# Attention weights change partitions through DRAM in 5 transfers a pair instead of 16, under a new order of all steps

## The chip, the cores and the metric

The kernel runs on one core of one Trainium2 chip. The metric is the device time of one execution in microseconds (us). Three runs of the kernel before took 381.66, 388.07 and 1155.09 us, with a median of 388.07 us. The execution that was profiled took 381.47 us; all rows below are from that one.

The core has five engines with a program of their own: TensorE (PE in the rows; PEld is its weight load), VectorE (DVE), ScalarE (ACT), GpSimd (POOL) and SyncE (SP). SP issues all the DMAs of this kernel. Each engine works through its instructions in the order in which they were written.

## The reference

```python
# attention: batch 4, 8 heads, 768 positions, head_dim 64, chunks of 32 positions, 8 memory keys
for c in range(nc):
    l_start, r_end = max(0, 32 * c - 16), min(S, 32 * c + 32 + 8)
    k_full = np.concatenate([mem_k, k[:, :, l_start:r_end]], axis=2)
    v_full = np.concatenate([mem_v, v[:, :, l_start:r_end]], axis=2)
    scores = scale * np.matmul(q_c, k_full.transpose(0, 1, 3, 2))
    a = np.exp(scores - np.max(scores, axis=-1, keepdims=True))
    a = a / (np.sum(a, axis=-1, keepdims=True) + 1e-09)
    out[:, :, 32 * c:32 * c + 32] = np.matmul(a, v_full)
# then x = that, as [batch, position, 512], and a gated block
h = gelu(x @ w_in)                                   # 512 -> 1024
u, v = h[..., :512], h[..., 512:]
v_n = (v - mean(v)) / np.sqrt(var(v) + 1e-06) * g_ln
v_s = np.einsum('ts,bsd->btd', w_sg, v_n) + b_sg[None, :, None]
return x + (u * v_s) @ w_out                         # 512 -> 512
```

All is float32. The large products run on TensorE as three products each of a high and a low part.

## The kernel before, in words

The work is cut into 24 attention units u: batch b = u // 6 and a tile of 128 positions, four chunks of 32. The names of steps below are those of the table ORDER (line 33), the letter or letters of a step with its unit or block behind them.

For each unit, **k** and **v** load its queries, keys and values (640 and 512 KB). **S** makes the scores on TensorE: 32 matmuls in the program, which the trace counts as 64, each with a weight load. **mx, sb, ex, sm, sr, nm** make the softmax on DVE, ACT and POOL; the weights of a unit stand in the tile `na`, 128 positions by 512. For the values they must stand with the keys on the partitions. Units 0 to 9 do that with four TensorE transposes (**T**) and a copy (**p**). Units 10 to 23, that is the pairs 5 to 11, do it in two moves: **yt** on DVE transposes blocks of 32 by 32 within their own 32 partitions into the tile `y`, and once both units of a pair are there, **Ea, Eb, Ec, Ed** bring the blocks to their partitions with four DMAs of 32 KB each, SBUF to SBUF (`pt<-y` in the rows). **A** then multiplies the weights in `pt` with the values: again 32 matmuls in the program and 64 in the trace, with as many weight loads. **xc, xh, xl** bring the result into the tiles `x` and `pair`.

The gated block follows for each batch: **V** (six) and **U** (eight) are the products with w_in, **W** (batch 0) or **P** (28 smaller products for each other batch) that with w_sg, **R** (14) that with w_out, **o** adds it to x, **out** stores a tile. **r, d** load and split the weights at the start. Blocks of w_sg and w_out that were prepared once go to DRAM (`blocks`, `outw`) and come back per batch into four ring tiles (**L**, 1152 KB each, and **M**, 512 KB each). An L or M waits until the product that last read its place in the ring has ended.

All steps stand in one hand-kept list. The loop at the end of `conformer_kernel` goes through ORDER and writes each step to its engine; a star chooses the step's second engine. Each engine, and the DMA queue on SP, keeps that order. What waits for what follows from the tiles. So the list decides what TensorE does next, and a DMA on SP whose wait isn't over holds up all DMAs listed behind it. The tiles `y` and `pt` exist once: E of a pair waits until A of the pair before has read `pt`, and the next yt waits until the transfers have read `y`.

Of the kernel before, what the change touches and what calls it, by code (L numbers as in the profile page):

```python
# [38 lines left out]
d2i01* S6 z5 d3i03 v500 d1i01 sr4 nm4* v502 vx00 d1i03 A3 v4 T4 vx02 vy02 sm5 d3i01 g31 p4 xc3 d4i03 d4i01 d4i00
xh3 d5i00 d4i02 xl3* sr5 nm5 Vb01 k7 v101 v602 S7 d5i01 A4 d6i01* k8 vy00 v600 d1o2* V03 mx7 d6i00* mx6 xh4 sb7  # L40
T5 d5i03 cb sb6 v702* v5 k9 g40 d5i02 ex6 d6i03* U001 xl4 v501 g01 p5 d2o2 d3o2 d6i02 v700* A5 v802 v6 xh5 v902*
d4o2 g00 Co10* xl5 g51 z6 ex7 S8 ga40 mx8 u1001 Co30 sm6 sm7 g50 v103 sr6 v800 V04 d5o2 Co20* d5o0 nm6 vx01
d6o2* v503 v7 g20 V05 k10 Co40* d6o0 v104 ga31 v900* v504 vy01 v105 v601 sr7 S9 sb8 v505 T6 ga21 hso0 lso0* nm7*
vx05 g10 xc4 mx9 g30 sb9 U011 v701* ga30 vx04 k11 U010 gb40 vx03 u1011 ex8 S10 Y00 xc5 p6* ex9 ro1 sm8 T7 vy03
v603 ga20 v703 g41 gb20* ga50 U002 sr8 vy05 p7 ga10 v803 mx10 vy04 U013 nm8 gb10* v605 v903* v604 d2o1 u1013
sb10 k12 ga00 u1002 gb50* d3o1 Y01 A6 v8 v705 v704* d1o1* sm9 v805 gb30 A7 gb00* xc6 ro3 gb31* v905* S12 v9 ga01
v801 g11 U003 T8 d4o1 v901* v804 N1 u1003 v904* d1o3 d5o1 U000 u1000 d2o3 ga11 d3o3 u1010 d4o3 d5o3 W002 W003
ga51 Co11 Co21 p8 Co31* d6o3* Co41 sr9 N0 Ga0 d6o1 nm9* hso1 W000 gb01 lso1* w1002 w2002 w1000 xc7 gb21* ga41
S11 Y10 Gd0 mx11 Gc0 sb11 A8 gb41 ex11 w1003 gb11 Gb0 Y11 H30 H10 gb51 I10 H20 W001 J10* w1001 k13 Ga1 I30 w2003
I20 H40* w2000 ex10 M01 W010 I40 sm10 J20 z11 Gb1 T9 U012 J40 sr10 Gd1 w3003 K20 xc8 nm10* w1010 Gc1 mx12 p9  # L50
sb12 w2001 u1012 sm11 w3001 K10 W012 J30 M06 ex12 H31* w2010 w3002 sr11 I31 H11* w3000 I11 w1012 w4002* yt10 H21
H41 I41 K30 w4000* K40 nm11 Ht100 It100 w4003* I21 M00 v10 M03 W013 w4001 W011 J21 J11 J41* A9 k14 w2012 Gb2
w1013 Gc2 J31 Ht300* w1011 yt11 Gd2 w2011 S13 K21 w2013 R100 Ed5 Ht101 R101 Ga2 It101 R201 o101 o201 o100 w3013
R200 o200 K41 Jt100 K31 w3012 K11 Jt101 Ec5 xh7 R501 xh6 o501 Ht301 xh8 w4013 k15 R500 w4012 Ht200* R301 o500
o301 z12 sm12 H32 M04 H12 S14 xl7* Ea5 xl6 R300 o300 sr12 I32 It200 I12 J32 V10 v110 mx14 V11 Ht201* It201 J12*
xl8* V12 Jt200* k16 H22 H42* I22 I42 nm12 sb14 Jt201* J42 v112 K12 v111 Eb5 v512 v511 Ht400* ex14 R600 J22 vx12
R601 K32 K42 M05 v510 vx11 It300 K22 o600 U101 S16 Jt300 Ht401 sm14 It301 A10 mx13 sb13 Jt301 o601 vy12 sr14
vy11 U102 vx10 ex13 It401 sm13 It400 M02 mx16 Jt400 Jt401* R700 o700 yt12 R701 R400 o701 R401 u1102 k18 v611
o400 S15 v11 out000 out001 o401 mx15 sr13 nm13 yt13 v711* U103 u1103 U100 v612 out002 out003 xc9 xh9 A11 vy10
sb15 xl9* xc11 nm14 out011 C311 sb16 v12 xh11 v610 xl11* xc10 xh10 xl10* V13 v113 out012 U111 u1100 v710* ex16  # L60
v513 C310* vx13 V14 L10 vy13 v613 v713 C110 C210 ex15 v813 sm15 k17 Ed6 C410 v810 v712 v910* sr15 S18 S17 mx17
v114 v913* v514 vx14 V15 Ec6 U110 sm16 out013 out010 vy14 v614 Ea6 v115 v515 v13 vx15 U112 vy15 v714 Eb6 L13
hs10 L11 ls10* u1112 v615 u1110 A13 C111 C312 v715 C112* v812 C211 v811 yt14 nm15 u1111 v815 C212 v912 A12 sr16
u1101 v911* sb17 v15 v814 C411* U113 u1113 P110 k19 yt15 ex17 v914* C412* v915* k20 P111 Q111 P210 P211 S19 L14
hs12 Q110 z17 L15 sm17 ls12 w1101 mx18 hs11 ls11 P611 P610 Q611 w2101 w3101 Q610 w4101* P711 Q711 P710 w1100
w2100 w3100 Ea7 w4100* P511 w1113 P510 nm16* sr17 sb18 Q710 xc12 w1112 w2113* P311 w2112* ex18 w3112 L16 xc13
w3113 P310 w1111 w2111 w1110 Ec7 w2110 M10 w4113* mx19 P411 Ht111* It111 Ht110* It110 R111 P410 Ht311 It311 M13
S20 Ht310* Eb7 Ed7 w1103 A15 v14 Jt111 yt16 w1102 M11 A14 nm17* w2103 w3103 Jt110* M16 yt17 k22 w2102 It310
Ht211* R110 It211 w4112 xc14 Ht210 k21 R510 w4103 o510 R511 w3102 R310 Jt310 sb19 w4102 o511 o110 o310 R311 M14
z18 N2 R211 It210 o311 R210 Jt210* Ed8 Ht410* M12 It410 xh12 xh14 xh13 Jt211 S21 o111 o211 xl12* R611 M15 R610  # L70
o210 V20 v120 xl14* xl13 V21 mx20 o610 v520 Ht411* Ea8 v17 sm18 sr18 It411 Jt410 Eb8 o611 Jt311 R710 o710 v121
v521 R711 Ec8 o711 Jt411 R410 R411 vx21 V22 vx20 nm18* U200 vy20 v620 o410 o411 sb20 ex20 out101 ex19 v122 v16
yt18 sm19 sr19 out100 mx21 v720* out113 C320 out102 out103 xc15 xh15 xl15* S22 A17 A16 nm19* V23 vy21 L21 v621
# [20 lines left out]
It231 Jt231 w4302 out212 Jt130* R130 M33 M31 w1303 w2303 R531 It331 o131 o531 R530 It330 M36 o530 M34 R331 R330
w3303 w4303 M35 Ht230 It230 Jt230 o331 R231 o130 Ht431 M32 o330 R630 R631 o231 out301 R230 o630 out310 Jt331
Jt330* R730 o631 o230 Ht430* o730 It431 Jt431 It430 R731 o731 Jt430 R430 R431 out300 out311 out312 out313 o430
out302 o431 out303
"""


# [831 lines left out]
```

## Time and profile before

| what | value |
|---|---|
| runs | 381.66, 388.07, 1155.09 us |
| the profiled execution | 381.47 us, its span 379.6 us |
| mean granted clock of TensorE | 0.986 |
| TensorE busy | 349.2 us, 92% of the span |
| weight loads busy (beside the matmuls) | 324.2 us, 85% |
| DVE, ACT, POOL busy | 266.5, 175.2, 202.5 us |
| chain that ended last | PE 80%, DMA 9%, issue 3%, ACT 3%, DVE 3% |
| DMA | 100.60 MB, mean 265 GB/s |

The span runs from the first to the last instruction; the execution's own time lies 1.9 us above it. The chain is followed back from the last instruction, at each step to what released it. "Issue" is time in which an engine waited for nothing that the profile shows. The granted clock is 1.00 at 2.4 GHz and 0.50 at 1.2 GHz.

### The profile page before, as it was taken

What the parts mean: (1) busy time and instruction counts of PE and PEld (TensorE: products, weight loads), DVE (VectorE), ACT (ScalarE), POOL (GpSimd) and SP (SyncE); (2) the same over time, 40 slices, a digit from 0 to 9 for tenths busy, and PEclk for the clock granted to TensorE, in tenths of its full rate; (3) what the DMA queues carried; (4) which work ended last, traced back from release to release, by engine and by line L of the source; (5) the groups of instructions that cost most, each with busy time, mean ns of one, the idle gap of its engine ahead of it and who ended that gap; (6) DMA issues with size and microseconds to landing.
All of it is one profiled execution on the core that took longest, in us unless ns stands there. A gap on an engine that the chain in (4) does not pass through costs nothing.

```text
span 379.6 us, 11105 instructions
## 1 busy us (share of the span) xinstructions
PE 349.2 (92%) x4678; PEld 324.2 (85%) x4678; DVE 266.5 (70%) x474; ACT 175.2 (46%) x299; POOL 202.5 (53%) x212
## 2 busy tenths in 40 slices
PE   2469989999999999999997995999999999999996
PEld 1349878889999888899987894899999998899996
DVE  2599998958788767795693773477477752655794
ACT  2366878745744543753251452774323423441140
POOL 1445877926848546065285551357348253452593
PEclk9999999999999999999998997899999999999999
DMA  7999688998996898489877677561994579008854
GB/s 272 355 372 382 230 298 273 305 354 302 329 376 241 281 350 308 149 319 385 306 265 268 210 214 294 197 246 39 325 377 177 182 233 403 12 0 310 318 174 169
DMA packets 33729, 100.60 MB, mean 265 GB/s; under 512 B 5264, under 2 KB 16016, under 8 KB 30736
## 3 DMA queue, kind: packets, MB, share of 16 engines
q1 hardware_dynamic: 33680, 99.90, 73.7%
q8 instruction: 37, 0.61, 0.7%
q14 instruction: 12, 0.10, 0.1%
HBM read 77.99 MB, written 18.22 MB: 253 GB/s over the span
## 4 chain that ended last, share of the span: by engine, by line
PE 80%; DMA 9%; issue 3%; ACT 3%; DVE 3%; POOL 2%; SPq 0%; ACTq 0%; POOLq 0%
PE mmc L109 19%; PE mmb L109 18%; PE mmd L109 17%; PE mma L109 16%; PE av L109 6%; PE s L109 4%; DMA qka<-in_qks 3%; DMA rawc<-in_w_in 2%; DMA ringa<-blocks 2%; DMA work<-in_w_out 2%; POOL gd L109 1%; ACT L109 1%; DVE mxb L109 1%; POOL work L109 0%; DVE ea L109 0%
## 5 line engine op out<-in xcount | busy, mean ns | idle before, releaser
L109 ACT ACT_TABLE_LOAD x24 | 30.8, 1283 | 5.5 <-DVE ea L109 2.8
L109 POOL TENSOR_TENSOR sums<-work,sums 128x384 fp32r<-128x384 f32 (+2 forms) x15 | 18.6, 1255 | 11.5 <-ACT sums L109 11.4
L109 ACT CAST sums<-work 128x384 fp32r<-128x384 f32 (+3 forms) x25 | 16.1, 662 | 13.2 <-DVE work L109 9.8
L109 PE MATMUL s<-qka 64*32 64x64 f32 x768 | 11.4, 246 | 7.7 <-DMA qka<-in_qks 6.8
L109 PEld LDWEIGHTS s<-qka 64*32 64x32 f32 x768 | 9.3, 116 | 10.0 <-DMA qka<-in_qks 4.7
L109 PE MATMUL av<-pt,vb 64*64 64x32 f32 x704 | 13.2, 220 | 4.1 <-issue 4.1
L109 PEld LDWEIGHTS av<-pt,vb 64*64 64x64 f32 x704 | 11.9, 135 | 5.6 <-issue 5.2
L109 PEld LDWEIGHTS av<-pt,va 64*64 64x64 f32 x768 | 13.6, 142 | 3.3 <-ACT pt L109 1.7
L109 PE MATMUL av<-pt,va 64*64 64x32 f32 x768 | 14.9, 226 | 1.4 <-ACT pt L109 1.4
L109 ACT ACTIVATE ea<-ea 128x512 f32<-128x512 f32 x12 | 7.6, 633 | 13.1 <-DVE ea L109 13.0
L109 POOL TENSOR_TENSOR work<-work 128x384 f32<-128x384 f32 (+1 forms) x6 | 6.7, 1109 | 11.8 <-DMA uh<-in_w_sgT 7.5
L109 POOL TENSOR_SCALAR rsb<-mvb 128x1 f32<-128x1 f32 x8 | 2.4, 299 | 19.3 <-DVE mvb L109 15.6
L109 PE MATMUL s<-qkb 64*32 64x64 f32 x704 | 10.1, 240 | 2.3 <-DVE ea L109 1.5
L109 PEld LDWEIGHTS s<-qkb 64*32 64x32 f32 x704 | 8.3, 112 | 4.4 <-DVE ea L109 1.8
L109 DVE TENSOR_TENSOR sums<-work,sums 128x768 fp32r<-128x768 f32 (+2 forms) x10 | 9.7, 966 | 2.1 <-ACT sums L109 2.1
L109 DVE STREAM_TRANSPOSE y<-na 128x512 f32<-128x512 f32 x14 | 9.9, 704 | 0.3 <-DMA qka<-in_qks 0.2
L109 PE MATMUL mmb<-w_in_hi,pairb 128*128 128x512 f32 x32 | 10.0, 439 | 0.0
L109 PE MATMUL mmd<-w_in_hi,paira 128*128 128x512 f32 (+1 forms) x40 | 10.0, 376 | 0.0
L109 DVE TENSOR_REDUCE mxa<-s 128x8 f32<-128x512 f32 x8 | 5.4, 677 | 6.3 <-PE s L109 6.3
L109 POOL TENSOR_SCALAR rsa<-mva 128x1 f32<-128x1 f32 x8 | 1.8, 224 | 14.8 <-DVE mva L109 14.5
L109 ACT ACTIVATE eb<-eb 128x512 f32<-128x512 f32 x12 | 7.5, 629 | 3.9 <-DVE eb L109 3.9
L109 PE MATMUL mmc<-w_in_hi,paira 128*128 128x512 f32 (+1 forms) x40 | 9.2, 351 | 0.0
(773 smaller groups left out, 1226.8 us busy)
## 6 DMA issues: line engine op xcount, KB each, us to landing
qka<-in_qks SPq DMA_DIRECT2D x12, 640.0 KB, 6.8
qkb<-in_qks SPq DMA_DIRECT2D x11, 640.0 KB, 6.2
ringd<-blocks SPq DMA_DIRECT2D x6, 1152.0 KB, 6.8
ringb<-blocks SPq DMA_DIRECT2D x6, 1152.0 KB, 6.7
va<-in_vs SPq DMA_DIRECT2D x12, 512.0 KB, 5.7
ringa<-blocks SPq DMA_DIRECT2D x5, 1152.0 KB, 6.5
vb<-in_vs SPq DMA_DIRECT2D x11, 512.0 KB, 5.2
ringa<-outw SPq DMA_DIRECT2D x11, 512.0 KB, 6.0
```

What stands on the lines that cost most here:

```text
L109: return self.tc.keep_in_program_order(getattr(self.engine, name)(*args, **kw))
```

## The change

Two things change. First, the four steps Ea to Ed of a pair (16 DMAs) become two: **X** writes the tile `y` to a DRAM tile `exch` of the pair's own, with four DMAs of 128 KB, and **E** reads it back into `pt` with one DMA of 512 KB. Second, the list ORDER is another one throughout, and the second engine is chosen for other steps. The products are the same.

```diff
+    exch = {p: dram.tile([P, 4, 256], F32, name=f"exch{p}") for p in range(PAIRS // 2, B * NTT // 2)}
...
-            def exchange(c):
-                def does(eng):
-                    for h in range(2):
-                        for b_ in range(2):
-                            at = 64 * h + 32 * b_
-                            eng.dma_start(
-                                pt_all[at:at + 32, c], y_t[32 * c:32 * c + 32, h, b_]
-                            )
-                return does
-
             step(f"yt{u}", blocks, vector)
             if j:
-                for c in range(4):
-                    step(f"E{'abcd'[c]}{u // 2}", exchange(c), sync)
+                def spread(eng):
+                    for c in range(4):
+                        eng.dma_start(
+                            exch[u // 2][:, c].rearrange("(g p) n -> p g n", g=4),
+                            y_t[32 * c:32 * c + 32].rearrange("p h b j a q -> p (h b) (j a q)"),
+                        )
+
+                step(f"X{u // 2}", spread, sync)
+                step(f"E{u // 2}", lambda eng: eng.dma_start(
+                    pt_all.rearrange("p c j a q -> p (c j a q)"), exch[u // 2].rearrange("p c n -> p (c n)"),
+                ), sync)
...
-k0 S0 mx0 sb0 k1 S1 ex0 z0 ri11 d2i11 sm0 sr0 nm0* T0 k3 v0 p0 k2 d3i11 mx1 sb1 ri12 ex1 sm1 d1i12* S2 mx2 A0
+k0 S0 mx0 sb0 ex0 z0 sm0 sr0 k1 S1 ri10 nm0* mx1 d1i10 sb1 ex1 T0 ri13 k2 p0 sm1 sr1 d2i13 d3i13 nm1* T1 p1
```

**First place: TensorE, before the second w_out products of batch 1.** S20, A15 and A14 stood in a row before (`s` and `av` are the tiles of the scores and of the values; an `x32` there is 64 in the trace):

```order
L109 MATMUL mmc<-ringb,vhf 128x384
L109 MATMUL s<-qkb 32x64 x32
L109 MATMUL av<-pt,va 64x32 x32
L109 MATMUL av<-pt,vb 64x32 x32
L109 MATMUL mmb<-paira,ringd 128x384 x6
```

Now S20 and A15, and S21 and A14, have products R between them:

```order
L108 MATMUL s<-qkb 32x64 x32
L108 MATMUL av<-pt,va 64x32 x32
L108 MATMUL mmd<-paira,ringd 128x384 x6
...
L108 MATMUL s<-qka 32x64 x32
L108 MATMUL av<-pt,vb 64x32 x32
L108 MATMUL mmc<-sums,ringd 128x384 x6
```

Five R of six matmuls each stand between the two.

**Second place: TensorE, in the w_in products of batch 2.** S22, A17 and A16 stood in a row before:

```order
L109 MATMUL mmc<-paira,w_in_hi 128x384 x8
L109 MATMUL s<-qkb 32x64 x32
L109 MATMUL av<-pt,va 64x32 x32
L109 MATMUL av<-pt,vb 64x32 x32
L109 MATMUL mmb<-w_in_hi,pairb 128x512 x4
```

and the same three stand in a row now, with A16 and A17 ahead of S22:

```order
L108 MATMUL mmb<-paira,w_in_hi 128x384 x8
L108 MATMUL av<-pt,vb 64x32 x32
L108 MATMUL av<-pt,va 64x32 x32
L108 MATMUL s<-qkb 32x64 x32
L108 MATMUL mmc<-w_in_hi,pairb 128x512 x4
```

**Third place: SP, the exchange of pair 8, whose weights A16 and A17 read.** Before, its 16 transfers and what stood between them:

```order
L109 DMA pt<-y 32x256 x4
L109 DMA ringa<-outw 128x1024
L109 DMA ringd<-outw 128x1024
L109 DMA pt<-y 32x256 x4
L109 DMA va<-in_vs 128x1024
L109 DMA pt<-y 32x256 x8
```

Now X8, three DMAs, E8, and what follows up to X9:

```order
L108 DMA exch_159<-y 32x4x256 x4
L108 DMA vb<-in_vs 128x1024
L108 DMA out<-xc 128x384
L108 DMA qka<-in_qks 128x1280
L108 DMA pt<-exch_159 128x1024
L108 DMA out<-xc 128x384 x2
L108 DMA va<-in_vs 128x1024
L108 DMA out<-xc 128x384
L108 DMA blocks<-ringc 128x2304
L108 DMA va<-in_vs 128x1024
```

At the start of the program SP's list moves too: before, the load k5 stood behind 7 weight and value loads and five k (7424 KB with it); now 9664 KB stand up to and with it, because all four tiles ri10 to ri13, ri00, ri02, ri03 and three v are ahead of it. A1 and the first half of V00 moved ahead of S5 on TensorE.

## Rows read from the trace of the kernel before

**Rows 1.** The page: engines' busy us (share) x instructions; DMA queue; chain by engine.

```profile
PE 349.2 (92%) x4678; PEld 324.2 (85%) x4678; DVE 266.5 (70%) x474; ACT 175.2 (46%) x299; POOL 202.5 (53%) x212
...
q8 instruction: 37, 0.61, 0.7%
...
PE 80%; DMA 9%; issue 3%; ACT 3%; DVE 3%; POOL 2%; SPq 0%; ACTq 0%; POOLq 0%
```

**Rows 2.** Windows: stretch, length, busy us (x instructions) by engine, clock, DMA share, GB/s.

```profile
0.00:20.00 20.00, 7.85 (x359) 6.70 (x361) 9.23 (x16) 6.40 (x10) 5.43 (x13) 1.00 0.87 318
20.00:40.00 20.00, 16.32 (x380) 14.79 (x362) 19.26 (x34) 13.12 (x23) 10.82 (x9) 1.00 0.95 360
...
200.00:220.00 20.00, 18.16 (x145) 16.71 (x146) 10.62 (x18) 5.25 (x9) 10.84 (x12) 0.91 0.61 217
```

**Rows 3.** Timeline of PE, 194.9 to 202: start, us, what, [idle before, releaser].

```profile
194.92 0.86 PE L109 MATMUL s<-qkb 64*32 64x64 f32 x64
195.71 1.24 PE L109 MATMUL av<-pt,va 64*64 64x32 f32 x61
...
196.80 1.15 PE L109 MATMUL av<-pt,vb 64*64 64x32 f32 x63
...
201.84 1.16 PE L109 MATMUL mmb<-paira,ringd 128*128 128x384 f32 x3 [3.18 <-issue]
```

**Rows 4.** Timeline of PE, 228.1 to 236.

```profile
228.95 1.41 PE L109 MATMUL av<-pt,va 64*64 64x32 f32 x61
...
230.20 1.14 PE L109 MATMUL av<-pt,vb 64*64 64x32 f32 x61
...
235.47 0.42 PE L109 MATMUL av<-pt,vb 64*64 64x32 f32 x2 [4.13 <-issue]
```

**Rows 5.** Windows behind the two stalls, for the clock.

```profile
201.84:205.30 3.46, 3.46 (x11) 3.46 (x12) 0.33 (x1) 0.51 (x1) 2.27 (x4) 0.53 0.39 120
...
232.80:235.47 2.67, 0.00 (x1) 0.01 (x1) 0.00 (x0) 0.00 (x0) 0.00 (x0) 0.50 0.77 301
235.47:239.60 4.13, 4.13 (x11) 3.29 (x12) 0.74 (x1) 2.31 (x4) 1.28 (x1) 0.50 0.19 57
```

**Rows 6.** Windows cut at the two stalls, for the count of instructions.

```profile
0.00:201.80 201.80, 179.20 (x3143) 164.34 (x3143) 156.47 (x280) 109.27 (x188) 115.58 (x120) 1.00 0.86 308
201.80:235.40 33.60, 29.50 (x377) 27.05 (x377) 20.18 (x36) 10.47 (x15) 13.80 (x16) 0.91 0.73 250
```

**Rows 7.** Timeline of PE, 166 to 168.5: two value steps in a row.

```profile
166.18 1.17 PE L109 MATMUL av<-pt,va 64*64 64x32 f32 x63
...
167.16 1.14 PE L109 MATMUL av<-pt,vb 64*64 64x32 f32 x63
168.22 0.44 PE L109 MATMUL mma<-pairb,w_in_lo 128*128 128x384 f32 x1
```

**Rows 8.** Tile pt, its transfers: SP's time for one issue, ns min/median/max.

```profile
L109 SPq DMA_DIRECT2D pt<-y x112: 507/588/1638, 114.1 to 305.1; - x112
```

**Rows 9.** DMA issues: what, queue, count, KB each, median us from issue to landing.

```profile
ringb<-blocks SPq DMA_DIRECT2D x6, 1152.0 KB, 6.7
va<-in_vs SPq DMA_DIRECT2D x12, 512.0 KB, 5.7
...
blocks<-sums SPq DMA_DIRECT2D x12, 384.0 KB, 4.7
pt<-y SPq DMA_DIRECT2D x112, 32.0 KB, 3.4
```

**Rows 10.** Chain of waits, 284 to 288: start, us, what: a product P, a product R.

```profile
284.54 1.59 PE mmc L109 x9
286.13 1.05 PE mma L109 x6
```

**Rows 11.** Timeline of PE, 26 to 34: S5, which waits for k5's load, and A1.

```profile
26.55 1.17 PE L109 MATMUL s<-qka 64*32 64x64 f32 x64 [2.14 <-DMA qka<-in_qks]
...
31.96 1.14 PE L109 MATMUL av<-pt,vb 64*64 64x32 f32 x64
```

More of the change, by code (lines that the diff above doesn't have):

```diff
@@ L39 @@
[L39 to L73, printed above, removed]
@@ L94 @@
[L94 to L97, printed above, removed]
+k0 S0 mx0 sb0 ex0 z0 sm0 sr0 k1 S1 ri10 nm0* mx1 d1i10 sb1 ex1 T0 ri13 k2 p0 sm1 sr1 d2i13 d3i13 nm1* T1 p1
+d1i13* d4i13 g01 d2i10 S2 mx2 v1 v0 sb2 A1 A0 ri11 k3 d2i11* xc1 d3i11 d3i10 d4i10 ex2 sm2 ri12 d5i13 S3 k4
@@ new lines @@
+d6i13* S4 d1i11 d5i10 d2i12* d3i12 d6i10 xh0 xl0 ro0 d1i12* sr2 xc0 d1o0 ri02 d2o0 d4i11 mx3 sb3 d5i11 v2 xh1
+nm2* T2 d2i02* xl1* d3o0 ri03 d6i11 ri00 d1i00* p2 ex3 A2 sm3 k5 sr3 d2i00* g10 mx4 g51 d2i03* ro2 nm3* Va00 sb4
+d4i12 d5i12 ex4 S5 g21 xh2 d6i12* Vb00 ri01 T3 d4o0 xl2 v100 d3i02 Va02 Vb02 sm4 d3i00 d3i03 d4i00 d1i03* d4i03
+sr4 nm4* p3 v3 mx5 v500 Va01 vx00 sb5 T4 d1i01* d2i01* v102 v502 d5i03 k7 A3 ex5 v4 d3i01 z5 d1o2 sm5 sr5 xc3 S7
+Vb01 nm5 k6 v5 xh3 vx02 vy02 d4i01 d5i00 xl3* v602 vy00 d1i02* d2o2* d6i00* g11 v702 d3o2 p4 xc2 v600 d5i01 S6
@@ new lines @@
+mx6 v802 d6i01* d4i02 T5 sb6 V03 d6i03 p5 d5i02 ex6 z6 g30 mx7 d6i02* g50 ga10 sm6 sb7 v700 sr6 A4 A5 xh5 v902
+xh4 xl4 d4o2 ex7 v101 Co30 Co10 U001 k8 v103 S8 xl5 g20 Co20 V04 gb10* d5o2 nm6 k9 S9 T6 d6o2* ga20 v800 Co40*
+g31 v501 v6 hso0 lso0 vx01 vy01 v601 v503 v900 ga30 mx8 sb8 g40 U013 gb30 sm7 v104 cb v701 d5o0 ga50 V05 k10
+d6o0 p6 ex8 U000 sm8 g00 vx03 xc5 u1001 S10 v504 sr7 sr8 nm7* v105 v7 gb20* v801 vx04 v901* gb50 vy04 vy03 ro1
+ga31 k11 d1o1 u1013 ga00 d2o1* v604 U011 ga40 mx9 Y01 v505 g41 u1011 U003 d3o1 Y00 ro3 vx05 v704 v804 d4o1 v603
@@ new lines @@
+w3003 w4003 W010 J20 Gb1 I40 w1010 w2010 xc7 K30 nm11* yt11 mx12 Gd1 J40 w2002 W012 Ht100* xc8 w1012 w4001* p9
+w3002 w4002* K20 U012 W013 H31 M03 S13 A9 u1012 w2012 I31 H11* I11 Gc1 H21 It100 v10 I21 J31* R100 Jt100* R101
+w1013 sb12 H41 J21 w2013 o101 w3013 R201 J11 o201 R200 o100 o200 Ht101* X5 It101 xh6 w3012 Jt101 k14 w4013 xh8
+R500 o500 Ga2 k15 R501 w4012 ex12 Ht301 S14 Ht201* Gb2 o501 I41 K40 R300 xh7 xl6* Gd2 R301 o300 J41 mx13 H32
+o301 H12* xl8* K11 xl7 I12 J12* I32 mx14 M04 V10 v110 K31 K21 H22 V12 Ht300 Gc2 I22 v510 J32 Ht200* v112 v512
@@ new lines @@
+u1100 vy13 C310 u1103 v613 ex15 v713 sm15 V14 ex16 C110* mx18 C210 L11 v712* v813 v13 v810 v910* U110 C410 U111
+v114 v913* v514 U113 k17 v115 S17 v515 vx14 vx15 hs10 vy14 v614 ls10* E6 A13 out013 v714 L10 k20 C312 vy15 C111
+C211 L13 v615 v715 U112 C112* C212* v811 yt14 sr15 C411 v812 v912* v911 nm15 C412* v12 xc13 u1113 yt15 P111 v815
+u1111 u1110 k19 v814 u1112 hs11 v914* hs12 X7 mx17 v915 P110 ls11 Q110 P210 Q111 w1100 sb17 w2100 w3100 w4100*
+ls12 P211 ex17 A12 S19 sm16 P610 P611 sr16 L14 nm16 xc12 L15 Q610 Q611 w1101 P710 w2101* Q710 mx19 v15 L16 P711
@@ new lines @@
+Q711 P510 sb18 z17 w1112 w2112* P511 w1113 P310 sm17 w3112 w1110 w2110 w3101 P311 w4101 sr17 P410 w1111 Ht110
+It110 w4112 P411 w2111 Ht111 It111 M10 R111 w1102 w2102 w3102 S20 w2113 Ht310* Jt110 Ht210* Jt111 w1103 M13 yt16
+E7 A15 w2103 Ht311 w3113 mx20 It311 It210 It310 R110 R511 w4113 o511 o111 R510 M16 o510 nm17* R311 w4102 Ht211*
+M11 ex18 z18 sb19 v14 sm18 R310 w3103 It211 Jt211* k21 o311 M14 S21 Jt311 Jt210 M15 w4103 Ht411* Jt310 It411 A14
+sr18 o310 xc14 k22 R611 Ht410* M12 R211 yt17 X8 It410 o110 R610 v16 ex19 R210 xh12 o611 o610 R711 o210 R710
@@ new lines @@
+xl12* nm18* Jt410* o711 xh13 xl13 Jt411 xh14 V20 R411 out100 xl14* k23 sb20 o710 o411 R410 v120 o410 mx21 o211
+E8 out102 yt18 ex20 V21 v121 v520 V22 v122 U203 vx20 vy20 sm19 v522 vx22 v521 vx21 vy22 v622 U202 v722 out103
+v17 out101 xc15 N2 v620 sr19 nm19 sb21 A16 A17 xh15 vy21 xc16 v19 S22 xl15 xh16 V23 u1203 sm20 sr20 yt19 X9 v720
+xc17 xh17 xl16* V24 xl17* v123 nm20 v523 v621 U210 ex21 out113 v721* vx23 v18 vy23 mx22 out110 u1202 v623 v723
+v823 C320* C120 U200 C220 v820 sb22 ex22 u1200 S23 yt20 C420 v923* sm21 v124 sr21 nm21 L24 V25 v524 yt21 vx24
@@ new lines @@
+v920 vy24 hs20 E9 U212 v125 sm22 v525 U213 L20 out112 u1212 mx23 sb23 ls20 L21 vx25 C322 U201 v624 v724 vy25
+U211 u1210 X10 C321 ex23 A19 u1201 C121* C221 v625 v725 C122 C222 C422 v821 v921* u1213 v822 u1211 hs22 v824
+v922* C421* v924* v825 hs21 A18 P120 P121 z23 L23 sr22 v925 v21 out111 ls22* P220 L25 P221 xc19 Q120 ls21 Q121
+w1200 w2200* P621 Q621 w3200 sm23 w4200 L22 P620 Q620 nm22* P721 P720 w1201 P520 Q720 L26 w2201 Q721 w3201 w1212
+w2212 w3212 w4212 E10 sr23 P521 P320 w1213 w2213* w1210 w2210 w3213 Ht120 It120 P321 w1211 P421 xc18 w4201 M20
@@ new lines @@
+L36 P731 P730 P531 Q731 P530 w4300* w1313 Q730 w1312 w2313* w2312 P331 w1311 w3312 P330 w3313 out212 w2311
+w4313* M30 Ht131 w4312 Ht331 It131 w1310 M33 P430 out211 P431 Jt131 w2310 Ht130 M36 w1302 w2302 Ht330* w1303
+It130 M31 w3302 Jt130 w4302 w2303 R130 Ht231* R131 R530 w3303 It330 M34 It231 Ht230 R531 w4303 M35 o530 It331
+R330 o531 R331 o130 o330 Jt231* R230 It230 Jt230 Ht430* o230 o131 M32 R630 Jt330 o331 R231 o630 out310 R631 o231
+Jt331* o631 R730 o730 R731 Ht431* It431 It430 Jt430 Jt431* o731 out301 R430 out300 o430 out311 out313 out312
@@ L98 @@
+out302 R431 o431 out303
 """
```

44 lines of the change are left out of this document (20 added, 24 removed).

## Prediction, made before the changed kernel had run

> **What bounds the kernel now.** I read the page's busy times first, then the chain, then windows of 20 us, and the timeline of TensorE where a window showed it idle. The reader is to see in [rows 1] that TensorE works 349.2 of 379.6 us and that 80% of the chain is its own work. The change leaves every product as it is, so what it can win or lose is TensorE's idle time, 30 us, and what a lower clock costs. Idle are 379.6 - 349.2 = 30.4 us. Of these 12.15 and 3.68 us lie in the first two windows of 20 us, where the DMA engines are 87 and 95% busy [rows 2], and 3.18 and 4.13 us in two stalls near 200 and 232 us [rows 3, 4]. The other 7.3 us are spread over the program and its last transfers.
>
> Both stalls have "issue" as releaser, so nothing that the profile follows was late. Each comes at the end of, or just behind, three steps S, A, A in a row. Such a step has 64 matmuls and 64 weight loads and takes 0.8 to 1.1 us: about 128 x 3 = 384 instructions within 2.9 us. Between 200 and 220 us, where products run, it is 291 instructions in 18 us [rows 2]. My reading is that TensorE had run out of instructions. The rows for it: queue q8 brought 37 packets of 0.61 MB together, so 16 KB each [rows 1]; TensorE has 2 x 4678 = 9356 instructions, 253 for a packet; and between the two stalls lie 2 x 377 = 754 of them [rows 6], 2.98 packets. Two stalls a whole number of packets apart look like borders of packets. Two value steps in a row went through without idle [rows 7]. Behind each stall the clock fell to its lower level: 0.53 over 3.46 us, and 0.50 over 4.13 us [rows 5], against 1.00 over all 201.8 us before [rows 6]. Work at half clock over t costs t/2, so 1.6 and 2.1 us. The first stall's bill is 3.2 + 1.6 = **4.8 us**, the second's 4.1 + 2.1 = **6.2 us**.
>
> The Trainium skill, page "Runtime: NRT & Kernel Launch", section "Instruction fetch mechanics", says that each engine streams its instructions in 16 KiB blocks and that crossing a border is mostly hidden. The 16 KB packets agree with these rows, the hiding not at these two places; by the rule the stalls have another cause and stay, which is a rival below.
>
> **The change part by part.**
>
> *The first triple is taken apart.* S20, A15 and A14 now have five products R between A15 and S21, some 5 us of TensorE, and another follows A14. What is left are pairs, and a pair ran without idle [rows 7]. So the first stall goes, with its clock: **-4.8 us**. Bounds: -4.8, and 0 if the cause isn't the density.
>
> *The second triple stays.* A16, A17, S22 stand in a row at nearly the same count of instructions. At worst it costs the same, 0; at best it goes, -6.2. The two stalls differ by 1 us, and in both the DMA engines were busy while TensorE waited (0.77 in the last stretch of the second, [rows 5]). In the new list the write of a ring to DRAM (1152 KB) and a load of values stand between E8 and A17, so the engines may have less to do by then, or as much. I take **-2 us**, nearer to "the same", since the three steps themselves are the same.
>
> *New dense places.* S7, Vb01, S6 stand close early (0.8 + 1.4 + 0.8 us for 280 instructions), and S2, A1, A0, S3, S4 in a row at the start. At the start each of these waits for a load of its own anyway. For the first place the nearest rows are the pair, 0, and the larger stall with its clock, +6.2. I take **+1 us**, nearer to the pair.
>
> *Start.* k5 has 9664 KB up to and with it instead of 7424, so 2.29 MB more; at 318 to 360 GB/s [rows 2] that is 6.4 to 7.2 us. S5 began at 26.55 us on its load [rows 11]. SP now issues the first nine loads without a wait, where before k3 stood fourth and waited for S0; the DMA engines stood idle 13% of the first 20 us [rows 2], so at most 2.6 us come back: S5 at 30 to 34 us (26.55 + 6.4 - 2.6 to 26.55 + 7.2). But A1 and the first half of V00, which ended behind it, at 33.1 us for A1 [rows 11], now lie ahead of it, so S5's end at 33.1 is the point of no change: between -2 and +2 us. I take **0**: in these 40 us the same DMA engines are at 91%, and VectorE works 28.5 of the 40 us [rows 2]; another order doesn't give the DMA engines more room.
>
> *The exchange itself.* 77 DMA issues fewer at 0.588 us [rows 8] free 45 us of SP's queue. TensorE waited for none of them by name, so this saves nothing on the path. Latency: sixteen issues take 9.4 us, and 3.4 to the last landing [rows 8, 9], together 12.8 us. Now four issues (2.4 us), a write to DRAM that lands in about 4.7 us (the nearest row that writes DRAM from SBUF, blocks<-sums with three times the bytes of one of the four), and a load of 512 KB, 5.7 us (va) [rows 9]: 12.8 us again. What hides it is TensorE's other work between E and A. SP runs ahead of the list, so I looked for what truly holds E: that A of the pair before has read `pt`, that X has landed, and that the DMAs listed ahead could go. The shortest case is E7: M13 stands ahead of it and waits for P711. From the end of P711 to A15, the first to read this pair's weights, stand P511, P510, P311, P310, P411, P410, R111 and S20, six P of 1.6 us, an R of 1.0 [rows 10] and an S of 0.9: 11.5 us of TensorE for a load of 5.7 us. The others have as much or more. **0**, bounds 0 and the price of the slow rival below. If that cover were gone, each us missing would be a us of TensorE.
>
> The Trainium skill, page "DMA: Bandwidth & Descriptors", section "Anatomy of one DMA", says of a similar path that most of a DMA's fixed cost is the wait for the write receipt, longest where DRAM is the target, which speaks against going through DRAM. The rows agree in direction (4.7 against 3.4 us); by it the exchange would be longer by one such receipt, and the sum would be unchanged as long as the cover holds.
>
> *The ring loads.* The shortest time between the product that frees a place and the one that reads it grows for L from 7.0 to 8.1 us of TensorE (a load takes 6.7, [rows 9]), and falls for one M from 7.0 to 6.0 (512 KB, 5.7; both counted in steps of [rows 10]). One M has 5.2 us in both lists. **0**; bounds -0.5 and +1.
>
> *VectorE, ScalarE, GpSimd.* Seven steps leave VectorE, four go to POOL, three to ACT; all three are below 71% [rows 1]. **0**, -1 to +2.
>
> Sum: 381.5 - 4.8 - 2 + 1 = 375.7, so **376 us**. The execution profiled, 381.47, stands 1.9 us above its span and 1.7% below the median of the three runs shown, 388.07; it lies with the lowest, 381.66, and the forecast is for such runs.
>
> **The rivals.**
>
> 1. *Likeliest, 376 us.* The first stall goes, the second is there at some length. With the second between 0 and -4 and the start between -2 and +2: 371 to 379. Chance 0.47.
> 2. *Both go.* At A16, A17, S22 the next packet comes in time or so soon that the clock holds. 381.5 - 4.8 - 6.2 = 370.5; with -2 at the start, 368.5. For it: the loads behind A17 can't be issued before A17 ends, so fewer are in flight. Against: three steps in 2.9 us are as dense as ever. 0.27.
> 3. *The stall moves.* S7, Vb01, S6 takes 6.2 and the second stays: 381.5 - 4.8 + 6.2 = 383; with +2 at the start 385. 0.12.
> 4. *The order has nothing to do with the stalls* (as the page on the runtime has it): both stay, 381.5. 0.04.
> 5. *Slower: the exchange holds up SP's queue.* E must wait on SP until X has landed; all listed behind it waits as well. Behind E6 to E9 stand k, v, L or M within three to five places. Price: 4.7 us each time less what stands between X and E; where nothing hides it, an L that had 8.1 - 6.7 = 1.4 us to spare is late by up to 3.3 us, once or more for each of batches 1 to 3 and its pairs, so some 4 x 3.3 = 13 us, and 381.5 - 4.8 + 13 = 390. It decides from where X to E holds more than 1.4 us of SP in front of an L. Against it: X is issued as soon as yt is done, well ahead in most pairs, and between X and E stand two to twelve other DMAs. 0.10.
>
> **How the numbers follow.** What a measurement of this kernel can tell from no change is about 2%, so below 373.9 is faster and above 389.1 slower. Faster: nearly all of rival 2 (0.25) and a fifth of the likeliest (0.10): 0.35. Slower: rival 5 and the tail of 3: 0.12. Within: 0.53. The range 368 to 386 leaves out rival 5 (0.10), the last of 3 (0.02) and the lowest of 2 (0.05), where the other terms are at their low bounds too. The likeliest's own range is 371 to 379.
>
> **What would show it.** In the changed kernel's profile: no "issue" idle over 1 us behind A15 or A14, clock 1.00 there; an "issue" idle of 1 to 4 us within or behind A16, A17, S22; TensorE idle of 14 to 18 us in the first 40; landing of `pt<-exch` before each A, with no idle of PE on it; 35 transfers instead of 112. I am wrong if "issue" idle stands elsewhere (S7 to S6 first), if PE waits by name for `pt<-exch` or a ring, or if the total idle falls though both stalls are there.

## The result, and the profile of the changed kernel

The changed kernel took 371.65 us (median of 4 runs, 371.48 to 372.11). The runs of before beside it took 381.66, 384.7 and 388.07 us (one of 1155.09 is an outlier). The ratio is 0.970, 95% interval 0.963 to 0.977: faster. The prediction was 376, range 368 to 386, with no measurable change as the likeliest outcome (0.53) and rival 2, "both go", at 370.5 (0.27). What came is rival 2, with a rest of the second stall.

The page of the changed kernel, the lines that answer to [rows 1]:

```profile
PE 346.8 (94%) x4678; PEld 321.0 (87%) x4678; DVE 273.7 (74%) x467; ACT 179.0 (48%) x304; POOL 206.3 (56%) x216
...
q8 instruction: 37, 0.61, 0.6%
...
PE 80%; DVE 10%; POOL 4%; DMA 2%; issue 2%; ACT 1%; SPq 0%; POOLq 0%; DVEq 0%
```

The profiled execution took 371.48 us, 9.99 less than that of before. TensorE's idle time fell from 30.4 to 369.7 - 346.8 = 22.9 us, so by 7.5; its busy time fell by 2.4, at the same count of instructions. Windows, columns as in [rows 2]:

```profile
0.00:20.00 20.00, 9.84 (x349) 8.17 (x350) 10.36 (x17) 5.71 (x9) 5.03 (x13) 1.00 0.91 357
20.00:40.00 20.00, 14.61 (x305) 13.48 (x305) 17.83 (x30) 13.88 (x24) 11.39 (x9) 1.00 0.92 324
200.00:220.00 20.00, 19.48 (x216) 16.94 (x215) 15.82 (x25) 9.90 (x14) 10.35 (x12) 1.00 0.76 250
...
228.97:233.00 4.03, 4.03 (x24) 3.25 (x24) 1.38 (x4) 1.47 (x4) 0.00 (x0) 1.00 0.86 275
```

The first 40 us have 15.6 us of idle, as before (15.8). The clock is 1.00 everywhere, and between 200 and 220 us TensorE is idle 0.5 us. The timeline of PE where [rows 3, 4] had the two stalls, start, us, what, and the idle ahead of it in brackets:

```profile
194.36 1.13 PE L108 MATMUL av<-pt,va 64*64 64x32 f32 x64
195.43 1.31 PE L108 MATMUL mmd<-paira,ringd 128*128 128x384 f32 x6
...
200.84 0.86 PE L108 MATMUL s<-qka 64*32 64x64 f32 x64
201.63 1.14 PE L108 MATMUL av<-pt,vb 64*64 64x32 f32 x64
...
224.92 1.14 PE L108 MATMUL av<-pt,vb 64*64 64x32 f32 x64
225.87 1.11 PE L108 MATMUL av<-pt,va 64*64 64x32 f32 x64
226.92 0.79 PE L108 MATMUL s<-qkb 64*32 64x64 f32 x56
228.97 0.32 PE L108 MATMUL s<-qkb 64*32 64x64 f32 x8 [1.27 <-issue]
```

Nothing is left of the first stall. Of the second, 1.27 us stand in S22, with no fall of the clock behind it. The exchange has 35 transfers, landing as follows (what, queue, count, KB each, median us from issue to landing); TensorE waits for neither by name:

```profile
exch<-y SPq DMA_DIRECT2D x28, 128.0 KB, 3.6
pt<-exch SPq DMA_DIRECT2D x7, 512.0 KB, 7.0
```

### The profile page after: what moved, and what is told of

Its sections match the earlier page's. It is cut to its first block, busy times and chain, and to the rows that moved or that the text cites. A ratio compares the mean times of both kernels' runs of the same rounds, so it can differ in the third digit from the quotient of the medians.

```text
span 369.7 us, 10990 instructions
## 1 busy us (share of the span) xinstructions
PE 346.8 (94%) x4678; PEld 321.0 (87%) x4678; DVE 273.7 (74%) x467; ACT 179.0 (48%) x304; POOL 206.3 (56%) x216
## 4 chain that ended last, share of the span: by engine, by line
PE 80%; DVE 10%; POOL 4%; DMA 2%; issue 2%; ACT 1%; SPq 0%; POOLq 0%; DVEq 0%
PE mmb L108 20%; PE mma L108 18%; PE mmd L108 18%; PE mmc L108 15%; PE av L108 6%; PE s L108 3%; POOL pairb L108 1%; POOL na L108 1%; DMA ue<-in_w_sgT 1%; DMA qka<-in_qks 1%; DVE rda L108 1%; DVE paira L108 1%; DVE sums L108 1%; DVE work L108 1%; DVE ea L108 1%
## 5 line engine op out<-in xcount | busy, mean ns | idle before, releaser
L108 POOL TENSOR_TENSOR sums<-work,sums 128x384 fp32r<-128x384 f32 (+3 forms) x17 | 25.3, 1498 | 5.3 <-ACT sums L108 5.2
L108 ACT COPY xa<-av 128x512 f32<-128x512 f32 x9 | 5.2, 585 | 13.5 <-DVE na L108 5.8
L108 PE MATMUL mma<-w_in_hi,pairb 128*128 128x512 f32 x40 | 11.4, 405 | 0.3 <-DVE pairb L108 0.3
L108 PE MATMUL mmb<-w_in_hi,paira 128*128 128x512 f32 (+1 forms) x48 | 11.5, 360 | 0.0
L108 POOL TENSOR_TENSOR work<-work 128x384 f32<-128x384 f32 (+1 forms) x6 | 5.5, 923 | 7.9 <-DVE work L108 7.0
L108 DVE TENSOR_TENSOR sums<-work,sums 128x384 fp32r<-128x384 f32 (+3 forms) x8 | 8.7, 1093 | 0.9 <-ACT sums L108 0.9
L108 PE MATMUL mmd<-pairb,w_in_hi 128*128 128x384 f32 x48 | 9.3, 336 | 0.0
```

Source lines behind the costliest of these rows:

```text
L108: return self.tc.keep_in_program_order(getattr(self.engine, name)(*args, **kw))
```

## What was tested

Theory 1, mine: TensorE ran out of instructions where 256 of them (a packet of 16 KB, below also a piece) are run through faster than the next packet comes, and the new order avoids that. The place where one piece ends and the next begins is called a border. Theory 2: the smaller exchange as such gave the gain. Theory 3: the order did, wherever a packet ends. To place the borders I counted TensorE's instructions in the compiled kernels: a 64-row matmul is two matmuls and two weight loads, and each wait beyond the one that an instruction can carry is one more. The traces bear the count out: between the two stalls of before lie the 754 matmuls and weight loads of [rows 6] and 14 such waits, 768 = 3 x 256. Counted in this way from each trace's start, all 31 places where TensorE idles over 0.3 us on "issue" in the fourteen traces of this document stand at place 192 or 193 of 256. Borders below are computed with that.

### Moving the borders alone

The kernel before with tiny matmuls that nothing reads, in two amounts. (Each is 4 instructions.)

```
+ tensor.matmul(mms.free[0][0:32, 0:16], ident[0:64, 0:32], ident[0:64, 0:16], start=True, stop=True)   # x n
  224:  x20 ahead of S0, x18 ahead of T0, x18 ahead of S2
  256:  64 of them at the same three places
```

> The kernel before, its order of steps untouched, with 56 tiny extra matmuls (64x32 by 64x16 of the identity, into a free PSUM tile, never read) put into the idle stretches ahead of S0, T0 and S2. They add 224 instructions to TensorE's stream and no work that anything waits for, so that every later instruction keeps its neighbours but stands 224 places further along. Theory 1 (the two stalls after 193 and 227 us are TensorE waiting for the next piece of its own instruction stream, and sit where a border of 256 instructions falls into a dense group of 64-row steps): both borders move into sparser steps, no issue idle over 1 us at either place, both stretches at a granted clock of 0.9 or more, and 370.5 us (369 to 373). Theory 2 (fewer transfers on the exchange gave the gain) and theory 3 (the order of the steps around the stalls, wherever a border falls): nothing changes, stalls of 3.2 and 4.1 us remain, 381.5 us (380 to 387).

> The same as the run with 56 extra matmuls, with 64 of them at the same three places: 256 instructions instead of 224, so that borders of 256 instructions fall where they fell before. It is the control for the extra matmuls themselves. Theory 1: the two stalls stay at the same two steps with 3.2 and 4.1 us (1 us either way) and the drop of the granted clock behind them, 381.5 us (380 to 387). If the extra matmuls did anything else (warming TensorE, another start), this run would move as the other does. Theories 2 and 3: also 381.5 us, so that only the pair of runs tells theory 1 from them.

Measured: 378.96 us with 224 instructions (ratio 0.986, 0.981 to 0.991) and 384.86 with 256 (1.007, 1.003 to 1.011), so that the extra matmuls as such cost a little and the place of the borders 5.9 us. With 256 (an execution of 388.55 us), PE's two stalls are at the same matmuls:

```profile
208.87 1.18 PE L46 MATMUL mmb<-paira,ringd 128*128 128x384 f32 x3 [2.65 <-issue]
...
241.84 0.42 PE L46 MATMUL av<-pt,vb 64*64 64x32 f32 x2 [3.43 <-issue]
```

With 224 both are gone; 0.62 us are left among the R, which the trace puts to a step of VectorE, and 0.85 in U201. But at the start there are new ones, where a border now falls into other dense steps:

```profile
23.52 0.65 PE L46 MATMUL s<-qkb 64*32 64x64 f32 x23 [2.91 <-issue]
...
33.26 1.08 PE L46 MATMUL av<-pt,y 64*64 64x32 f32 x32 [3.58 <-issue]
```

So the border decides where a stall stands, and theory 3 in its plain form falls. The total of 370.5 was missed, because I had looked at the late borders alone: the trace stands 5.2 us behind before by 70 us and 6.4 by the first of the two places, and gains 9.3 from there to behind the second.

### The exchange alone

The order of before, with the 4 writes and 1 read of the changed kernel.

```
- ... Ea5 ... Eb5 ... Ec5 ... Ed5 ...     (each 4 transfers pt<-y)
+ ... X5 at the first of these places, E5 at the last ...    (5 to 11)
```

> The kernel before with the changed kernel's exchange alone: 4 writes to the scratch at the place of the first group of the old transfers, 1 read at the place of the last, 35 transfers in all instead of 112; the order of every other step is that of before. Theory 1: the stalls sit in TensorE's stream, which has not changed, so that they remain at the same two steps: 381.5 us (378 to 387; the 3 us below, because SP and the DMA engines are less loaded at the second stall). Theory 2: the gain comes along, 371.5 us (370 to 374). Theory 3: 381.5 us.

Measured: **371.04 us, ratio 0.9715 (0.966 to 0.977)**. Theory 2 had it and mine didn't: without the new order, the exchange gives the whole gain. Step by step against the trace of before, all of it comes at the two places: R110 to S21 takes 7.5 us instead of 12.5, the start of A16 to that of V23 1.05 instead of 5.6; up to the first place the two run within 1.1 us of each other. A smaller stall is left, in V23, where before lost about as much to the low clock:

```profile
228.92 1.21 PE L46 MATMUL mmb<-w_in_hi,pairb 128*128 128x512 f32 x4 [1.93 <-issue]
```

So theory 1 was right on what was lost, and theory 2 on what took it away. How can the exchange move a stall of TensorE's stream? In two ways. Its 27 fewer waits move the borders, by 12 instructions at the first stall and 20 at the second. And SP, which was busy issuing, is free earlier. SP's timeline of before, then of this kernel:

```profile
187.37 5.03 SPq L109 DMA_DIRECT2D pt<-y  x8
192.44 0.58 SPq L109 DMA_DIRECT2D vb<-in_vs  x1
193.11 0.85 SPq L109 DMA_DIRECT2D ringa<-outw  x2
195.81 0.33 SPq L109 DMA_DIRECT2D qkb<-in_qks  x1
```

```profile
184.75 0.32 SPq L46 DMA_DIRECT2D pt<-exch  x1
185.12 0.60 SPq L46 DMA_DIRECT2D vb<-in_vs  x1
186.75 0.91 SPq L46 DMA_DIRECT2D ringa<-outw  x2
194.90 0.33 SPq L46 DMA_DIRECT2D qkb<-in_qks  x1
```

The same 1.5 MB of loads go out at 192.4 to 194.0 us before, at 185.1 to 187.7 here. The border in A15 is passed at 195.8 us before, at 194.9 here. Windows around it, of before and then of this kernel (the last three columns are clock, DMA share, GB/s):

```profile
194.00:195.80 1.80, 1.80 (x76) 1.45 (x76) 1.70 (x4) 0.39 (x1) 1.80 (x3) 1.00 0.97 335
195.80:199.50 3.70, 2.87 (x131) 2.50 (x131) 3.50 (x5) 2.48 (x6) 3.70 (x4) 1.00 1.02 403
```

```profile
194.00:195.00 1.00, 1.00 (x79) 0.90 (x80) 0.90 (x3) 0.00 (x0) 1.00 (x2) 1.00 0.10 41
195.00:196.80 1.80, 1.80 (x129) 1.76 (x121) 1.80 (x4) 0.93 (x2) 1.80 (x2) 1.00 0.52 102
```

In before the DMA engines are full, and the next packet of q8 starts 3.7 us after the border; here they are nearly idle, and it starts 0.7 us after it.

That gives theory 4: **a stall is the time from one border until the packet has come and TensorE goes on, less the time in which the 256 instructions up to the next border run.** Later kernels below test its two halves apart.

### Putting the borders back

```
  (the kernel of 371.04 us)
+ x4 of the tiny matmuls ahead of S16
```

> The order of before with the changed kernel's exchange alone (the run that gave 371.0 us), plus four tiny extra matmuls of the identity (64x32 by 64x16, 16 instructions in all, never read) ahead of S16. In that run TensorE's own stream was shorter by 27 instructions that only wait: an A step waits once for the one read of the scratch where it waited several times for the 16 transfers. So its borders of 256 instructions moved by 12 to 16 places at the two stalls. The four matmuls move them back to within a matmul of where they stood before: A15's second matmul and R110's third, A17's first and the last of A16. Theory 1, mended (the gain of the exchange is that shift and nothing else): both stalls return, 2.5 to 4.5 us of issue idle at R110 and 2.5 to 5 at the end of A16, with the drop of the clock, and 380 us (377 to 385). Theory 2 (16 transfers held up the DMA engines or SP, and TensorE's instructions with them): no stall returns over 2 us, 371 us (370 to 373.5).

Measured: 377.44 us (376.51 to 378.9), ratio 0.990 (0.983 to 0.997), so 16 instructions, which put both borders back to within four places, cost 6.4 of the 10.8 us. The second stall is back in full, with the clock at 0.83 over 220 to 240 us. The first is back by 0.87 us only:

```profile
200.08 0.97 PE L46 MATMUL mmb<-paira,ringd 128*128 128x384 f32 x4 [0.87 <-issue]
...
231.88 2.07 PE L46 MATMUL mmb<-w_in_hi,pairb 128*128 128x512 f32 x4 [4.01 <-DVE pairb L46]
```

The second row's releaser is misleading: in the kernel without the four matmuls V23 began at 224.86, while that same step of VectorE ended at 228.1. V23's first matmul is the border, and the next packet ended 1.45 us ahead of this restart. So both theories had half: the second stall hangs on the border, the first on the load as well. (A further 1.9 us of this one trace were lost at 82 us, where the two kernels differ in nothing but those matmuls later on: a product waits there for ScalarE to read its tile, and ScalarE had waited until 82.7 us, against 79.8 in the kernel without the matmuls, for a load of w_out. Why that load was late isn't shown.)

### Less load, more load

The kernel before, with the three loads ahead of the first border made small:

```
- step(f"v{u}", lambda eng: eng.dma_start(v, vs[b, tt]), sync)
+ cut = 1 if u == 14 else 4
+ step(f"v{u}", lambda eng: eng.dma_start(v[:, 0:cut], vs[b, tt][:, 0:cut]), sync)
  (M11 and M16 alike: 128 of 1024 columns)
```

> The kernel before, its order, its 16 transfers and all its waits kept, with three loads made small: the load of vb for A14 moves 128 KB instead of 512 KB, the two loads of ringa that SP issues right behind it 64 KB instead of 512 KB each. It leaves those parts of the operands stale, so that it computes something else in the same time. In the trace of before these three are issued at 192.4 to 194.0 us, behind 16 issues of the exchange that keep SP busy from 177.3 on, and their 1.5 MB move at 194 to 200 us, just when TensorE passes the border in A15 (195.8 us); the packet with its next instructions starts 3.7 us later. With the changed exchange and the same order they are issued at 185 to 187 us, are through by 194, and the packet starts 0.7 us after the border. Theory 4 (a stall is the time that the packet of instructions takes to come, longer behind other transfers, less the time that 256 instructions last): the packet starts within 1.5 us, the stall at R110 falls from 3.2 to 0 to 1.3 us, that at A16 stays at 4.1, and 377 us (375 to 379.5). Rival (the border alone decides, whatever the DMA engines carry): the stall at R110 stays at 3 us or more, 381.9 us (380 to 385).

Measured, PE's timeline at the two places:

```profile
203.65 0.80 PE L109 MATMUL mmb<-paira,ringd 128*128 128x384 f32 x3 [1.19 <-issue]
...
235.42 0.42 PE L109 MATMUL av<-pt,vb 64*64 64x32 f32 x2 [3.78 <-issue]
```

The packet starts 1.05 us after the border, the first stall falls to 1.2, the second stays: theory 4 at the place in question. The total does not follow: 382.78 us against 383.36 (0.994, 0.990 to 0.999). In the one trace S20 starts 3.8 us later than in before, and the stretch from there to behind the first stall gains 3.6. What is lost is lost ahead of the three loads (2.2 already by W012), so they can't have caused it; whether it is this run alone isn't settled.

The other way round, more load in the kernel that had none there:

```
  (the kernel of 371.04 us)
+ for i in range(4):
+     eng.dma_start(more_d[i], qks[i, 0])      # ahead of k22
```

> The order of before with the changed kernel's exchange (371.0 us), and four extra copies of 640 KB each from an input to DRAM scratch that nothing reads, issued on SP ahead of the load of qkb for S22, where SP otherwise has nothing to issue from 187.7 to 194.9 us. They keep the DMA engines busy when TensorE passes the border in A15 at 195 us; TensorE's stream and its borders stay as they were. Theory 4: the packet of instructions starts 3 to 5 us after the border instead of 0.7, a stall of 1.5 to 3.5 us of issue idle comes at R510, 374 us (372.5 to 378; the upper end with a fall of the clock, or where the loads for S21 come late). Rival (the border alone decides): no issue idle over 0.5 us at R510, 371 us (370 to 373).

Measured: 375.8 us (373.44 to 378.58), ratio 0.983 (0.974 to 0.992). This interval overlaps that of the kernel without the copies, so the trace has to decide. A stall is there, at the border in R510, where the kernel without the copies has none:

```profile
198.22 0.69 PE L46 MATMUL mmd<-pairb,ringd 128*128 128x384 f32 x3
201.47 0.69 PE L46 MATMUL mmd<-pairb,ringd 128*128 128x384 f32 x3 [2.56 <-POOL paira L46]
```

It stands between two matmuls of one product, which read the same tiles; the tile of the step named as releaser (`paira`) they don't read. TensorE's stream is the same in both kernels; the packet starts 3.6 us after the border instead of 0.7. The rival falls.

### The new order without the new exchange

```
  (the changed kernel)
- ... X8 ... E8 ...
+ first try:  Ea8 Eb8 Ec8 Ed8 at E8's place
+ second:     Ed8 Ec8 Ea8 Eb8 at X8's place (pairs 7 and 10: behind A12, A18)
```

> The changed kernel, its order of steps kept, with the old 16 transfers per pair of tiles back in place of the 5, all at the place where the read of the scratch stood. Theories 1 and 3: TensorE's stream is that of the changed kernel, so that the gain stays: 371.5 us (371 to 375; the 3.5 us above for 16 issues of about 0.6 us each on SP at one place, which delay loads queued behind them by up to 9 us). Theory 2: the gain goes, 381 us (379 to 390).

> The changed kernel's order with the old 16 transfers, each group at the first place where it finds its data and its target free: where the write to the scratch stood for pairs 5, 6, 8, 9 and 11, right behind A12 and A18 for pairs 7 and 10. (The first try of such a kernel put them where the read of the scratch stood, by when y is another tile's: it computed something else.) TensorE gets 11 waits more than the changed kernel, which move its borders by 1 to 5 matmuls and none of them into a denser place. Theory 1: 372 us (371 to 376; stalls of 1 to 4 us at A16 to S22 alone; the rest for SP, which waits at 7 places for the targets). Theory 2: 381 us (378 to 388).

Measured: 410.52 us (1.075, 1.068 to 1.081) and 416.52 (1.093, 1.087 to 1.100). In the first, `y` had been overwritten by a later tile, so `pt` got that tile's weights; TensorE waited 11.8 us for `pt<-y` by name. In the second SP stands still for 41.5 us until A steps have ended: 31.5 of them ahead of transfers `pt<-y`, until `pt` is free, the rest ahead of loads of values. Behind it stand ring loads, for which TensorE then waits:

```profile
SPq L46 <- PE av L46: 41.5, 8, 12.5
```

```profile
PE mmb L46 <- DMA ringd<-blocks: 21.5, 2, 12.2
```

The first expectation had nothing of that; the second had SP's waits, but at 4 us at most. The new order needs the scratch, which takes `y` before `pt` is free, so the totals don't tell the theories apart. The traces say a little: with 16 transfers under the new order TensorE has no "issue" idle behind A15 or A14, and 1.13 and 1.38 us in S22, as in the changed kernel. But the loads around these places come at other times too.

### The changed kernel with its borders moved

```
  (the changed kernel)
+ x20 of the tiny matmuls ahead of S5
```

> The changed kernel, its order and its 5 transfers kept, with 20 of the tiny extra matmuls (80 instructions) ahead of S5, where TensorE waits 4.7 us for a load. Borders of 256 instructions then stand 40 matmuls earlier, and three pieces are run through in about 2 us: the one that begins in A12 (175 us), in R310 (203 us) and in A16 (226 us). Theory 1 (a piece that is run through in less than the 3 to 6 us which the next one takes to come ends in a stall): new stalls of 1 to 4 us of issue idle at those three places, with falls of the granted clock behind some, and 379 us (374 to 387). Theory 2 (the exchange) and theory 3 (the new order as such): 371.6 us (371 to 373), no new stall over 1 us.

Measured: 376.18 us (375.45 to 377.15), ratio 0.9875 (0.982 to 0.993); so 80 instructions that nobody waits for take back 4.5 us. One of the three expected stalls came, at the end of A14, and the clock behind it fell (0.83 over 200 to 220 us); one of 0.78 us that I hadn't expected came at 56 us.

```profile
208.40 0.21 PE L46 MATMUL av<-pt,vb 64*64 64x32 f32 x1 [2.93 <-issue]
```

At the other two pieces the packet had started 2.25 and 0.61 us ahead of the first border, and nothing stalled. So a packet can be asked for before the border is executed, and my expectation lacked that. What decides how much earlier wasn't tested.

### Two tries at a better kernel

```
  a: the changed kernel     - U203 ... A16 A17 ... S22      + A16 A17 U203 ... S22
  b: before's order, new exchange   - U200 ... S22 A17 A16  + S22 A17 U200 A16
```

> The changed kernel with one step moved: U203, 24 matmul and weight-load instructions that run some 4 us, goes from ahead of A16 to between A17 and S22, so that no 256 instructions in a row are of 64-row steps there. Theory 1: the 1.27 us of issue idle in S22 go, 370.4 us (369.5 to 371.5), 1.2 us under the changed kernel. Theories 2 and 3: no change, 371.6 us (or up to 2 us more if A16, which comes 4 us sooner, waits for its read of the scratch).

> The order of before with the changed kernel's exchange (371.0 us), and one step moved: U200, 24 matmul and weight-load instructions of some 4 us, from ahead of S22 to between A17 and A16. In that run the piece between the borders in A17 and in V23 lasted 3.9 us, its packet of instructions started 3.4 us after the first border, took 1.0 and TensorE went on 1.4 us later, which left a stall of 1.9 us. With U200 inside the piece lasts 5.8 us. Theory 4: the stall there falls to between 0 and 0.5 us, 369.2 us (368 to 370.5). Rival (the stall belongs to the steps, or another border pays for it): 371 us (370 to 373). A loss of its own is possible where A16, which now ends 4 us later against S22, makes the steps that read it late: up to 2 us.

> The changed kernel as it is, beside these runs and so against the same runs of before: 371.6 us (371 to 372.5), 2.5 to 3% under before, by every theory. It is run for the comparison with the kernel whose U203 is moved (370.7 us).

Measured: (a) 370.74 us (369.24 to 371.25; ratio 0.9725, 0.968 to 0.977), the stall in S22 gone; the changed kernel again 372.13 (371.89 to 373.77; 0.9723, 0.967 to 0.977). It is lowest by its median, but the ratios don't tell the two apart. (b) 372.92 us (0.976, 0.970 to 0.981): the stall of 1.9 us is gone, but S22, which comes sooner, waits 1.15 us for the scores' tile. The stretch gains 0.6 us against the trace of the kernel before this change, and the span, 369.5 against 369.4, nothing. So theory 4 had the stall right, and the total of 369.2 was missed. A place where a step can wait for nothing but instructions is also one where it can wait for its data.

The repeat shows one more thing. Its stall in S22 was 1.46 instead of 1.27 us, and behind it the clock was low, where the first execution kept 1.00:

```profile
229.30:233.30 4.00, 4.00 (x18) 3.09 (x17) 1.29 (x2) 0.62 (x1) 0.00 (x0) 0.57 1.01 296
```

### All borders together

Read from the DMA records of each trace: us from the first border to the packet's start, the DMA engines' busy share in that time, how long the 256 instructions ran, the time between the starts of the two matmuls at the next border, and the time from the packet's end to TensorE's restart.

| kernel, first border | packet starts | DMA share | piece runs | gap | end to restart |
|---|---|---|---|---|---|
| before, A15 | 3.69 | 1.02 | 2.54 | 3.51 | 1.49 |
| before, A17 | 4.05 | 0.98 | 2.17 | 4.34 | 1.53 |
| 256 instructions more, A15 | 3.88 | 1.00 | 3.10 | 2.99 | 1.21 |
| 256 instructions more, A17 | 3.36 | 1.03 | 2.20 | 3.65 | 1.57 |
| small loads, A15 | 1.05 | 0.36 | 2.51 | 1.53 | 1.58 |
| small loads, A17 | 3.79 | 0.99 | 2.21 | 4.00 | 1.48 |
| exchange alone, A15 | 0.66 | 0.02 | 3.53 | none | |
| exchange alone, A17 | 3.44 | 1.02 | 3.59 | 2.33 | 1.52 |
| borders back, A15 | 0.78 | 0.07 | 2.27 | 1.20 | 1.55 |
| borders back, A17 | 3.66 | 1.02 | 1.85 | 4.23 | 1.45 |
| more load, A15 | 3.59 | 1.01 | 3.36 | 2.89 | 1.60 |
| changed, A16 | 0.71 | 0.00 | 1.74 | 1.48 | 1.53 |
| changed + 80, R310 | 2.91 | 1.04 | 1.97 | 3.15 | 1.28 |

The rows fall into two groups: with a DMA share of 0.36 or less the packet starts 0.7 to 1.1 us after the border, with 0.98 or more 2.9 to 4.1. These packets take 0.9 to 1.4 us. From border to restart, where there is a stall, that makes 3.2 us at the least (changed, A16) and 6.5 at most (before, A17). Where little but 64-row steps stands in a piece, it runs in 1.7 to 2.5 us.

## Why the prediction was half right

The time lies inside the range, but the forecast itself, no measurable change at 376, missed; what came is a rival with a chance of 0.27. The reading of the two stalls held. That the total came so near is partly luck, since the exchange, priced at 0, gives the same gain without the new order. Its steps in turn:

- *The first triple, -4.8.* The stall and its low clock went, as forecast. By the table the new order would do for that: the piece from the border in A15 on runs 6.8 us in the changed kernel, longer than the longest time from border to restart there, 6.5. But the order isn't needed, which I didn't see: with the exchange alone and the order of before the stall goes too, since the packet comes 3.0 us sooner.
- *The second triple, -2:* the term that was mis-sized. The stall fell from 4.13 to 1.27 and its 2.1 us of low clock went: 2.86 + 2.1 = **5.0 us**. The three steps are as dense as before, which I weighed; I gave too little weight to the packet. It started 0.71 us after the border, against 4.05 before. The DMA engines did nothing in that time, and were 25% busy over the whole stretch:

```profile
224.90:228.97 4.07, 2.81 (x185) 2.59 (x185) 3.28 (x6) 1.89 (x4) 3.61 (x3) 1.00 0.25 67
```

- *New dense places, +1.* S7 to S6 cost next to nothing: 2.92 us for the piece, and an idle of 0.17 at its end. There is a new 1.39 us at the start, in S3; the idle of the first 40 us is unchanged, so it cost nothing that can be seen. The second triple and this term, -3 and -1, make 4 of the 4.3 us by which 376 was too high. The two rows:

```profile
21.15 0.81 PE L108 MATMUL s<-qka 64*32 64x64 f32 x38 [1.39 <-issue]
...
44.79 0.24 PE L108 MATMUL s<-qkb 64*32 64x64 f32 x1 [0.17 <-issue]
```

- *The exchange itself, 0.* That step failed in its reason. I priced SP's 45 us and 77 transfers at nothing, since TensorE waited for none of them by name. It waited for them as "issue", through loads sent late that kept the packet waiting, and through waits in its own stream that set the borders (27 fewer with the exchange alone, 19 fewer in the changed kernel). The run with the exchange alone shows -10.8. The latency, 12.8 us by either way in the sum, came out near that (landings of 3.6 and 7.0 against 4.7 and 5.7), and TensorE waited for none of it.
- *Start, rings, other engines, 0.* As forecast: 15.6 us of idle in the first 40, and no wait of TensorE for a ring above 0.3 us.
- *Rivals.* "The stall moves" happened in the runs with extra matmuls. "Slower" didn't: SP waited 3.9 us for `exch<-y` in all. The rule of the Trainium skill behind rival 4 (page "Runtime: NRT & Kernel Launch", section "Instruction fetch mechanics": crossing a border is mostly hidden) holds for most of the 36 to 38 borders of each trace and fails at dense ones, with gaps of up to 4.3 us.

What stays open: how far ahead of execution a packet can be asked for, what the new order gives with the exchange as it was, and the losses ahead of S20 in two single traces.

## What to carry to other kernels

Where TensorE idles on "issue", count its instructions between such places, waits included. If it is a whole number of packets, there are three levers: put long-running instructions between dense steps, keep large loads from being issued just ahead of that border, and remember that any edit that adds or drops a wait moves every border behind it. So a change on another engine can gain or lose several us on TensorE without a row that names it; a handful of instructions that nobody needs, put ahead of it, is the test.

## What was not expected of the hardware

- Packets of instructions come later beside data: they start 0.7 us after a border with idle DMA engines and up to 4.05 us after it with full ones (the table). Adding 2.6 MB of copies to the same stream moved one from 0.66 to 3.59 us.
- Restart comes 1.2 to 1.6 us after the packet's end in every stall of the table.
- A stall's length alone doesn't decide whether the clock falls to its lower level. Stalls of 1.27 us (the changed kernel, S22), 1.93 (exchange alone, V23), 2.56 (more load, R510) and 3.58 us (224 instructions, at 33 us) left it at 1.00; one of 1.46 us in S22 was followed by 0.57 over 4 us, those of 3.2 and 4.1 us in before by 0.53 and 0.50.
